# Finding the 32nd score with a padded MAX8, and moving short-lived values into PSUM, in a fused attention, gMLP and MoE kernel

## The chip, the cores and the metric

The kernel runs on one core of one Trainium2 chip. The metric is device time in microseconds (us) of one execution. Engines: TensorE (PE; its weight loads are PEld), VectorE (DVE), ScalarE (ACT), GpSimd (POOL), and SyncE (SP), which only issues DMAs here.

## The reference, cut to what matters

```python
# attention: 2 batches, 8 heads, 576 positions, head dimension 64, all float32
scores = scale * np.matmul(q, k.transpose(0, 1, 3, 2))
kth = np.partition(scores, -32, axis=-1)[..., -32:-31]     # the 32nd largest of each row
scores = np.where(scores >= kth, scores, -1e9)
attn = exp(scores - max); attn = attn / (attn.sum(-1) + 1e-9)
x = (attn @ v)                                  # heads joined: (2, 576, 512)
# gMLP
h = gelu_tanh(x @ w_in); u, v = halves of h
v_s = einsum('ts,bsd->btd', w_sg, layernorm(v) * g_ln) + b_sg     # the "spread"
x = x + (u * v_s) @ w_out
# MoE: each token is sent to one of 8 experts, out = p[e] * relu(x @ w1[e]) @ w2[e]
```

What this case is about is `kth`: for each of 18,432 score rows the kernel needs the 32nd largest value, as the threshold of a mask.

## The kernel before, in words

The work of attention is cut into 72 **units**: a unit is 128 score rows of one head against all 576 keys (or 64 rows each of two heads). `body` walks the row tiles of batch 0 and then of batch 1; `unit` does one unit: `scores` (PE, L307, evacuated by ACT at L310 to `s_sb`), `weights_fast` (the top 32 and the softmax numerators), five transposes on PE (L377), their evacuation on ACT (L380), and ten half-products with V on PE (L385). After every unit `pump` places some steps of the other work in between, taken first in, first out from a list: the eight loads of `w_in` (`load_mlp`, `from_double`), then for every finished row tile the first gMLP product (`mlp_in`), then `spread(0)`, the loads of `w_out`, and the output steps. What is left of the list runs after the last unit. `experts` follows. A planner orders each engine's instructions at build time by priority and by its own estimates of time; on the chip each engine takes them in that order. There are three PSUM banks under the name `m_ps`, taken in turn by all of the work in between.

**The 32nd score, per unit (`weights_fast`).** DVE takes the top 8 of each of eight segments of 72 scores (L336), and then three rounds of MAX8 on the 64 candidates (L339), two MATCH_REPLACE8 between them (L341). The third round is `last8`, whose last value is the 24th score t. ACT takes the sign of t minus each score (L347), which leaves on the side a sum `cnt` = 576 - 2n, with n the number of scores at or above t (24 to 31 when all is well). POOL multiplies score by sign (L351): positive only for positive scores below t. DVE takes MAX8 of those (L353, tile `tb`), the 25th and following scores. The 32nd is the (32-n)th of these eight. DVE picks it (L356): it compares `cnt` with eight constants in `order`, multiplies the matches with `tb`, and sums into `kths`. This is one SCALAR_TENSOR_TENSOR with an accumulator, so that a DVE_READ_ACCUMULATOR follows. The mask is then made on DVE (L364, every other unit), or on ACT with a one-element DVE instruction ahead of it (L361, L362), and multiplied into the exponentials on POOL (L365).

**The weights (`from_double`, L187 on).** `w_in` and `w_out` arrive as 64-bit floats, in 12 pieces of 128 x 512. A piece lands in the raw tile `dbl` (one buffer). DVE shifts and joins the high and low words into a float32 magnitude (L194, L195) in an SBUF tile named `rest`, whose three buffers the units use too; ACT takes the absolute value (L196) and the sign of the high word (L197); POOL multiplies the two (L198).

**The spread.** `spread` evacuates a PSUM bank with one DVE instruction into an SBUF tile `vs` (L533) and multiplies `vs` into U (L537, and L542 for the rows that both batches share).

After attention, two DVE instructions (L1074, L1075) collect flags, over all 72 units, for rows in which the shortcut did not find the threshold; were one set, attention and the experts would be done again exactly, at the end.

Of the kernel before, what the change touches and what calls it, by code (L numbers as in the profile page):

```python
# [11 lines left out]
F32 = mybir.dt.float32  # L12
F32R = mybir.dt.float32r
BF16 = mybir.dt.bfloat16
I32 = mybir.dt.int32
U32 = mybir.dt.uint32
AF = mybir.ActivationFunctionType
OP = mybir.AluOpType
# [25 lines left out]
def tile_topk_gmlp_moe(  # L44
# [15 lines left out]
    nc = tc.nc  # L60
    B, H, D, S = qT.shape
    P = 128
    DM = H * D
# [3 lines left out]
    E, _, FE = w1.shape  # L67
    CE = FE // P
    TOP = 32
    NJ = (S + P - 1) // P  # L70
    LAST = S - (NJ - 1) * P
    HS = S // 2
# [11 lines left out]
    const = ctx.enter_context(tc.tile_pool(name="const", bufs=1))  # L84
# [67 lines left out]
    SEG = 8  # L152
    UNITS = B * (H * (NJ - 1) + H // 2)
    NG = 24
    order = const.tile([P, 8], F32, name="order")


    nc.vector.tensor_scalar(order, iota_e, 2.0, float(S - 2 * (TOP - 1)), op0=OP.mult, op1=OP.add)
    last8 = const.tile([P, UNITS, 8], F32, name="last8")
    kths = const.tile([P, UNITS], F32, name="kths")  # L160

    LESS = 1.0 + 2.0 ** -20

    def attention(fast):
# [21 lines left out]
        def from_double(dst, src):  # L186


            n = dst.shape[-1]
            hl = raw.tile([P, 2 * n], U32, name="dbl", bufs=1)  # L190
            nc.sync.dma_start(hl, src.bitcast(U32))
            l, h = hl[:, 0::2], hl[:, 1::2]
            a = wk.tile([P, n], U32, name="rest", bufs=3)
            nc.vector.tensor_scalar(a, h, 0x08000000, 3, op0=OP.bitwise_xor, op1=OP.logical_shift_left)  # L194
            nc.vector.scalar_tensor_tensor(a, l, 29, a, op0=OP.logical_shift_right, op1=OP.bitwise_or)  # L195
            nc.scalar.activation(a.bitcast(F32), a.bitcast(F32), AF.Abs)  # L196
            nc.scalar.activation(dst, h.bitcast(F32), AF.Sign)  # L197
            nc.gpsimd.tensor_tensor(dst, a.bitcast(F32), dst, op=OP.mult)  # L198

        def load_in(hf, c):  # L200
            from_double(w_in_sb[:, c, hf * F2:(hf + 1) * F2], w_in[c * P:(c + 1) * P, hf * F2:(hf + 1) * F2])
# [109 lines left out]
            return s_sb  # L311

        def weights_exact(s_sb):
            top = sm.tile([P, TOP], F32, name="top")
            rest = wk.tile([P, S], F32, name="rest", bufs=3)
            cur = s_sb
            for r in range(TOP // 8):
                t8 = top[:, r * 8:r * 8 + 8]
                nc.vector.max(t8, cur)
                if r < TOP // 8 - 1:  # L320
                    nc.vector.match_replace(rest, t8, cur, -3.0e38)
                    cur = rest
            nm = sm.tile([P, 1], F32, name="nm")
            nc.vector.tensor_scalar(nm, top[:, 0:1], -scale, None, op0=OP.mult)
            e_sb = wk.tile([P, S], F32, name="e_sb", bufs=5)
            nc.scalar.activation(e_sb, s_sb, AF.Exp, bias=nm, scale=scale)
            nc.vector.scalar_tensor_tensor(e_sb, s_sb, top[:, TOP - 1:TOP], e_sb, op0=OP.is_ge, op1=OP.mult)
            return e_sb

        def weights_fast(s_sb, un):  # L330


            w = S // SEG
            cand = sm.tile([P, 8 * SEG], F32, name="cand", bufs=4)
            for g in range(SEG):
                nc.vector.max(cand[:, 8 * g:8 * g + 8], s_sb[:, g * w:(g + 1) * w])  # L336
            for r in range(NG // 8):
                t8 = last8[:, un, :] if r == NG // 8 - 1 else sm.tile([P, 8], F32, name="ta", bufs=12)
                nc.vector.max(t8, cand)  # L339
                if r < NG // 8 - 1:  # L340
                    nc.vector.match_replace(cand, t8, cand, -3.0e38)  # L341
                if r == 0:
                    nm = sm.tile([P, 1], F32, name="nm")
                    nc.gpsimd.tensor_scalar(nm, t8[:, 0:1], -scale, None, op0=OP.mult)  # L344
            sg = wk.tile([P, S], BF16, name="sg", bufs=3)
            cnt = sm.tile([P, 1], F32, name="cnt")
            nc.scalar.activation(sg, s_sb, AF.Sign, bias=last8[:, un, 7:8], scale=-LESS, accum_out=cnt)  # L347
            e_sb = wk.tile([P, S], F32, name="e_sb", bufs=5)
            nc.scalar.activation(e_sb, s_sb, AF.Exp, bias=nm, scale=scale)  # L349
            below = wk.tile([P, S], F32, name="rest", bufs=3)  # L350
            nc.gpsimd.tensor_tensor(below, s_sb, sg, op=OP.mult)  # L351
            t8 = sm.tile([P, 8], F32, name="tb")
            nc.vector.max(t8, below)  # L353
            pick = sm.tile([P, 8], F32, name="pick")
            kth = kths[:, un:un + 1]
            nc.vector.scalar_tensor_tensor(pick, order, cnt, t8, op0=OP.is_equal, op1=OP.mult, accum_out=kth)  # L356
            mask = wk.tile([P, S], BF16, name="mask", bufs=2)
            if MASK[un % len(MASK)] == "a":

                ink = sm.tile([P, 1], F32, name="ink")  # L360
                nc.vector.tensor_scalar(ink, kth, -(1.0 - 2.0 ** -24), None, op0=OP.mult)  # L361
                nc.scalar.activation(mask, s_sb, AF.Sign, bias=ink)  # L362
            else:
                nc.vector.tensor_scalar(mask, s_sb, kth, None, op0=OP.is_ge)  # L364
            nc.gpsimd.tensor_tensor(e_sb, e_sb, mask, op=OP.mult)  # L365
            return e_sb
# [59 lines left out]
        def mlp_in(t):  # L426
# [13 lines left out]
            def v(c):  # L440
# [7 lines left out]
                with tc.high_priority(offset=EVAC):  # L448
                    vg = one.tile([P, F2], F32, name="row", bufs=3)
                    gelu = nc.scalar.activation(vg, ps["v"], AF.Gelu_apprx_tanh)  # L450
                    with tc.issue_after(gelu.ins):
                        nc.scalar.activation(UT[b][:, :, k * P:(k + 1) * P], ps["u"], AF.Gelu_apprx_tanh)
                    st = sm.tile([P, 6], F32, name="st")
                    nc.vector.bn_stats(st, vg)
                    mv = sm.tile([P, 2], F32, name="mv")
                    nc.vector.bn_aggr(mv, st)
                    ve = sm.tile([P, 1], F32, name="ve")
                    nc.vector.tensor_scalar(ve, mv[:, 1:2], 1e-6, None, op0=OP.add)
                    rs = sm.tile([P, 1], F32, name="rs")
                    nc.gpsimd.tensor_tensor(rs, ve, neghalf, op=OP.pow)  # L460
                    nc.vector.tensor_scalar(VN[b][:, k, :], vg, mv[:, 0:1], rs, op0=OP.subtract, op1=OP.mult)

# [49 lines left out]
        def spread(b):  # L512
# [3 lines left out]
            def step(f, n, j):  # L516
# [12 lines left out]
                if j != js[-1]:  # L529
                    return  # L530
                with tc.high_priority(offset=EVAC):
                    vs = one.tile([P, HS], F32, name="vs", bufs=2)
                    nc.vector.scalar_tensor_tensor(vs, ps[0], g_sb[:, f:f + 1], b_sg_sb[:, at], op0=OP.mult, op1=OP.add)  # L533
                    at = slice(at.start, min(at.stop, FULL))
                    m = at.stop - at.start
# [23 lines left out]

        def logits(b, fill, spare):  # L560

            added = raw.tile([P, 2 * DM], U32, name="dbl", bufs=1).bitcast(F32)[:E + 1, :S]
            both = slice(b * LAST, (b + 1) * LAST)
            for at, u in ((slice(FULL), UT[b]), (slice(FULL, S), UT[B][:, :, both])):
                ps = ps_m.tile([P, 512], F32, name="m_ps")
# [499 lines left out]
                give(slice(0, P), tq, pq)  # L1065
        own.close()

    zero = const.tile([1, DM], F32, name="zero")
    nc.vector.memset(zero, 0.0)
    nc.sync.dma_start(xrows[0:1], zero)  # L1070
    attention(True)

    fa = const.tile([P, UNITS], F32, name="fa")
    nc.vector.tensor_scalar(fa, kths, 1e-30, None, op0=OP.is_le)  # L1074
    nc.vector.scalar_tensor_tensor(fa, last8[:, :, 7], 0.0, fa, op0=OP.is_le, op1=OP.max)  # L1075
    fs = const.tile([P, 1], BF16, name="fs")
    nc.vector.tensor_reduce(fs, fa, axis=AX.X, op=OP.max)
    fi = const.tile([P, 1], I32, name="fi")
# [46 lines left out]
```

## Time and profile before

| | |
|---|---|
| three runs | 612.41, 610.81, 605.28 us; median 610.81 us |
| the profiled execution | 611.23 us, of which the span of instructions is 609.5 us |
| busy in the span | PE 551.0 us (90%), DVE 373.0 (61%), ACT 308.3 (51%), POOL 292.6 (48%) |
| mean granted clock of TensorE | 0.917 of 2.4 GHz |

The shares are means over stages that differ: attention with the work in between runs to about 350 us, the rest of the gMLP to about 440 us, and the experts from there to the end. PE's share includes time at half clock, and instructions that are recorded as busy while the engine is fed slowly.

### The profile page before, as it was taken

The numbers are of one execution on the slowest core, as the hardware profiler recorded it, in microseconds if no ns is written. First come the engines' busy times: TensorE is split into PE (matmuls) and PEld (weight loads), VectorE is DVE, ScalarE is ACT, GpSimd is POOL, SyncE is SP. The second block draws the span as 40 slices with busy tenths as digits, with TensorE's granted clock in tenths as the row PEclk, the third lists the DMA queues.
The fourth block names the chain that finished last, engine by engine and source line by source line (L and its number), as shares of the span: only waits on it lengthen the run. The fifth ranks groups of instructions, "written<-read, shape, count | busy, mean of one in ns | idle before, by whom it ended". The sixth has DMA issues, their size and how long they took to land. (4 is left out here: it accounts for less than half of the span.)

```text
span 609.5 us, 10453 instructions
## 1 busy us (share of the span) xinstructions
PE 551.0 (90%) x3430; PEld 458.6 (75%) x3430; DVE 373.0 (61%) x1765; ACT 308.3 (51%) x563; POOL 292.6 (48%) x330
## 2 busy tenths in 40 slices
PE   6778799999989969898897799999989999999993
PEld 3445667777778768767886478777768999999993
DVE  5889978898989999899899931234800111111110
ACT  3767756978989797866789523323010101111110
POOL 4488948676998858777567820170040102000010
PEclk9555758989999999999898799999999999999998
DMA  9963200000301101210020030000389998766001
GB/s 234 245 169 131 70 27 9 6 24 0 92 19 54 27 17 28 70 35 18 2 70 1 35 114 8 18 2 0 105 274 388 388 387 313 270 236 242 17 18 32
DMA packets 45668, 63.92 MB, mean 105 GB/s; under 512 B 14553, under 2 KB 20697, under 8 KB 45602
## 3 DMA queue, kind: packets, MB, share of 16 engines
q1 hardware_dynamic: 43938, 58.16, 29.6%
q0 software_dynamic: 1664, 4.97, 2.4%
q8 instruction: 30, 0.49, 0.3%
q14 instruction: 36, 0.29, 0.2%
HBM read 56.04 MB, written 7.33 MB: 104 GB/s over the span
## 5 line engine op out<-in xcount | busy, mean ns | idle before, releaser
L385 PE MATMUL pv<-v,pt 128*128 128x96 f32 (+1 forms) x720 | 113.2, 296 | 9.8 <-DVE row L401 6.0
L385 PEld LDWEIGHTS pv<-v,pt 128*128 128x128 f32 x720 | 106.7, 215 | 19.9 <-DVE row L401 7.3
L365 POOL TENSOR_TENSOR e_sb<-e_sb,mask 128x576 f32<-128x576 f32 x72 | 94.0, 1307 | 42.0 <-ACT e_sb L349 14.4
L351 POOL TENSOR_TENSOR rest<-s_sb,sg 128x576 f32<-128x576 f32 x72 | 93.1, 1297 | 20.6 <-ACT sg L347 19.8
L336 DVE MAX8 cand<-s_sb 128x8 f32<-128x72 f32 x576 | 89.6, 217 | 19.6 <-ACT s_sb L310 19.3
L307 PE MATMUL s_ps<-kk,qh 64*128 64x288 f32 (+1 forms) x224 | 80.4, 474 | 15.1 <-ACT s_sb L310 15.0
L377 PE MATMUL pt_ps<-ident,e_sb 128*128 128x128 f32 x360 | 73.6, 297 | 8.5 <-ACT pt L380 5.2
L968 PE MATMUL h_ps<-xw,w_sb 128*128 128x152 f32 (+6 forms) x512 | 76.5, 298 | 0.8 <-DMA w_sb<-in_w_dram 0.8
L979 PE MATMUL y_ps<-hT,w_sb 128*128 128x152 f32 (+6 forms) x512 | 75.3, 299 | 0.7 <-DMA w_sb<-in_w_dram 0.7
L968 PEld LDWEIGHTS h_ps<-xw,w_sb 128*128 128x128 f32 x512 | 71.4, 190 | 1.1 <-ACT hT L971 1.1
L979 PEld LDWEIGHTS y_ps<-hT,w_sb 128*128 128x128 f32 x512 | 71.0, 190 | 1.1 <-DMA w_sb<-in_w_dram 1.1
L307 PEld LDWEIGHTS s_ps<-kk,qh 64*128 64x128 f32 (+1 forms) x224 | 43.9, 224 | 32.7 <-ACT s_sb L310 21.6
L377 PEld LDWEIGHTS pt_ps<-ident,e_sb 128*128 128x128 f32 x360 | 51.8, 164 | 19.7 <-issue 11.0
L971 ACT ACTIVATE hT<-h_ps 128x152 f32<-128x152 f32 (+6 forms) x32 | 9.7, 302 | 112.7 <-PE h_ps L968 111.9
L347 ACT ACTIVATE sg<-s_sb,last 128x576 bf16<-128x576 f32 x72 | 55.6, 772 | 18.4 <-DVE last L339 14.0
L380 ACT ACTIVATE pt<-pt_ps 128x640 f32<-128x640 f32 x72 | 50.4, 700 | 25.4 <-PE pt_ps L377 24.4
L940 POOL DMA_INDIRECT out_dram<-orow,to x10 | 10.0, 1000 | 103.1 <-ACT orow L939 48.3
L349 ACT ACTIVATE e_sb<-s_sb,nm 128x576 f32<-128x576 f32 x72 | 55.7, 773 | 2.2 <-POOL nm L344 1.2
L310 ACT ACTIVATE s_sb<-s_ps 128x576 f32<-128x576 f32 x72 | 46.3, 642 | 18.6 <-PE s_ps L307 18.5
L973 DVE TENSOR_SCALAR hT<-h_ps 128x152 f32<-128x152 f32 (+6 forms) x32 | 10.3, 323 | 73.2 <-PE h_ps L968 67.7
L353 DVE MAX8 tb<-rest 128x8 f32<-128x576 f32 x72 | 53.6, 745 | 1.2 <-POOL rest L351 1.1
L981 DVE COPY yT<-y_ps 128x152 f32<-128x152 f32 (+6 forms) x32 | 9.9, 323 | 64.2 <-PE y_ps L979 64.2
(248 smaller groups left out, 919.7 us busy)
## 6 DMA issues: line engine op xcount, KB each, us to landing
w_sb<-in_w_dram SPq DMA_DIRECT2D x32, 1024.0 KB, 12.3
dbl<-in_w_in_dram SPq DMA_DIRECT2D x8, 512.0 KB, 4.6
kr<-in_kT_dram SPq DMA_DIRECT2D x16, 144.0 KB, 3.2
v<-in_v_dram SPq DMA_DIRECT2D x8, 256.0 KB, 5.4
dbl<-in_w_out_dram SPq DMA_DIRECT2D x4, 512.0 KB, 3.5
xin<-row SPq DMA_DIRECT2D x8, 256.0 KB, 2.3
qraw<-in_qT_dram SPq DMA_DIRECT2D x16, 128.0 KB, 2.8
back<-xin SPq DMA_DIRECT2D x8, 256.0 KB, 2.7
```

Of the source, the lines that this page charges most:

```text
L307: nc.tensor.matmul(s_ps[:, n, :HS], w, k[:, n * HS:(n + 1) * HS], start=m == 0, stop=m == len(terms) - 1)
L336: nc.vector.max(cand[:, 8 * g:8 * g + 8], s_sb[:, g * w:(g + 1) * w])
L347: nc.scalar.activation(sg, s_sb, AF.Sign, bias=last8[:, un, 7:8], scale=-LESS, accum_out=cnt)
L349: nc.scalar.activation(e_sb, s_sb, AF.Exp, bias=nm, scale=scale)
L351: nc.gpsimd.tensor_tensor(below, s_sb, sg, op=OP.mult)
L353: nc.vector.max(t8, below)
L365: nc.gpsimd.tensor_tensor(e_sb, e_sb, mask, op=OP.mult)
L377: tr = nc.tensor.transpose(pt_ps[:, t * P:(t + 1) * P], p_sb[:, k0:k0 + P], ident)
L380: nc.scalar.activation(pt.rearrange("p t q -> p (t q)"), pt_ps[:, :NJ * P], AF.Relu)
L385: nc.tensor.matmul(PV[b][:, i % g, :], pt[:, t, :], V1[b][:, t, w * i * (D + 1):w * i * (D + 1) + nv], start=t == 0, stop=t == NJ - 1)
L968: nc.tensor.matmul(hp[:, :W], w1_sb[:, c, f * P:(f + 1) * P], xw[:, c, at], start=c == 0, stop=c == CD - 1)
L979: nc.tensor.matmul(yp[:, :W], w2_sb[:, f, c * P:(c + 1) * P], hT[:, f, :W], start=f == 0, stop=f == CE - 1)
```

## The change

Five things change.

1. The pick goes. `rest` is seven columns wider; POOL writes into them (cnt + order) x -2^100, with `order` now 2i - 527, so that exactly n - 24 of the seven come out huge and positive, and the others negative. The eighth value of DVE's MAX8 over all 583 columns is then the 32nd score itself. `cnt` is kept for every unit, in `cnts`.
2. In `from_double` the joined words go to a PSUM bank of `m_ps` instead of an SBUF `rest`; ACT writes the absolute value straight to the destination, and the sign in place over the low words of the raw tile, with a stride of two.
3. `dbl` has two buffers. Some small tiles get fewer buffers.
4. `vs` is not a tile of its own any more: the evacuation of the spread writes into its PSUM bank in place, and the product with U reads it there.
5. The row of zeros is written from 128 partitions with 4 values each instead of one partition with 512. The flags get five more DVE instructions on 72 columns, since the pick did one of the tests on the way.

```diff
-    order = const.tile([P, 8], F32, name="order")
-    nc.vector.tensor_scalar(order, iota_e, 2.0, float(S - 2 * (TOP - 1)), op0=OP.mult, op1=OP.add)
+    ADD = TOP - NG - 1
+    order = const.tile([P, ADD], F32, name="order")
+    nc.vector.tensor_scalar(order, iota_e[:, :ADD], 2.0, float(2 * NG + 1 - S), op0=OP.mult, op1=OP.add)
     last8 = const.tile([P, UNITS, 8], F32, name="last8")
-    kths = const.tile([P, UNITS], F32, name="kths")
+    next8 = const.tile([P, UNITS, 8], F32, name="next8")
+    cnts = const.tile([P, UNITS], F32, name="cnts")
...
-            hl = raw.tile([P, 2 * n], U32, name="dbl", bufs=1)
+            hl = raw.tile([P, 2 * n], U32, name="dbl", bufs=2)
             nc.sync.dma_start(hl, src.bitcast(U32))
             l, h = hl[:, 0::2], hl[:, 1::2]
-            a = wk.tile([P, n], U32, name="rest", bufs=3)
+            a = ps_m.tile([P, n], F32, name="m_ps").bitcast(U32)
             nc.vector.tensor_scalar(a, h, 0x08000000, 3, op0=OP.bitwise_xor, op1=OP.logical_shift_left)
             nc.vector.scalar_tensor_tensor(a, l, 29, a, op0=OP.logical_shift_right, op1=OP.bitwise_or)
-            nc.scalar.activation(a.bitcast(F32), a.bitcast(F32), AF.Abs)
-            nc.scalar.activation(dst, h.bitcast(F32), AF.Sign)
-            nc.gpsimd.tensor_tensor(dst, a.bitcast(F32), dst, op=OP.mult)
+            nc.scalar.activation(dst, a.bitcast(F32), AF.Abs)
+            sign = l.bitcast(F32)
+            nc.scalar.activation(sign, h.bitcast(F32), AF.Sign)
+            nc.gpsimd.tensor_tensor(dst, dst, sign, op=OP.mult)
...
-                t8 = last8[:, un, :] if r == NG // 8 - 1 else sm.tile([P, 8], F32, name="ta", bufs=12)
+                t8 = last8[:, un, :] if r == NG // 8 - 1 else sm.tile([P, 8], F32, name="ta", bufs=8)
...
-            cnt = sm.tile([P, 1], F32, name="cnt")
+            cnt = cnts[:, un:un + 1]
             nc.scalar.activation(sg, s_sb, AF.Sign, bias=last8[:, un, 7:8], scale=-LESS, accum_out=cnt)
...
-            below = wk.tile([P, S], F32, name="rest", bufs=3)
-            nc.gpsimd.tensor_tensor(below, s_sb, sg, op=OP.mult)
-            t8 = sm.tile([P, 8], F32, name="tb")
-            nc.vector.max(t8, below)
-            pick = sm.tile([P, 8], F32, name="pick")
-            kth = kths[:, un:un + 1]
-            nc.vector.scalar_tensor_tensor(pick, order, cnt, t8, op0=OP.is_equal, op1=OP.mult, accum_out=kth)
+            below = wk.tile([P, S + ADD], F32, name="rest", bufs=3)
+            nc.gpsimd.tensor_tensor(below[:, :S], s_sb, sg, op=OP.mult)
+            nc.gpsimd.tensor_scalar(below[:, S:], order, cnt, -2.0 ** 100, op0=OP.add, op1=OP.mult)
+            nc.vector.max(next8[:, un, :], below)
+            kth = next8[:, un, 7:8]
...
-                    vs = one.tile([P, HS], F32, name="vs", bufs=2)
+                    vs = ps[0]
                     nc.vector.scalar_tensor_tensor(vs, ps[0], g_sb[:, f:f + 1], b_sg_sb[:, at], op0=OP.mult, op1=OP.add)
...
-            added = raw.tile([P, 2 * DM], U32, name="dbl", bufs=1).bitcast(F32)[:E + 1, :S]
+            added = raw.tile([P, 2 * DM], U32, name="dbl", bufs=2).bitcast(F32)[:E + 1, :S]
...
-    zero = const.tile([1, DM], F32, name="zero")
+    zero = const.tile([P, DM // P], F32, name="zero")
     nc.vector.memset(zero, 0.0)
-    nc.sync.dma_start(xrows[0:1], zero)
+    nc.sync.dma_start(xrows[0:1].rearrange("o (p f) -> p (o f)", p=P), zero)
     attention(True)
     fa = const.tile([P, UNITS], F32, name="fa")
-    nc.vector.tensor_scalar(fa, kths, 1e-30, None, op0=OP.is_le)
+    nc.vector.tensor_scalar(fa, next8[:, :, 7], 1e-30, None, op0=OP.is_le)
     nc.vector.scalar_tensor_tensor(fa, last8[:, :, 7], 0.0, fa, op0=OP.is_le, op1=OP.max)
+    fc = const.tile([P, UNITS], I32, name="fc")
+    nc.vector.tensor_scalar(fc, cnts, float(2 * TOP - 2 - S), None, op0=OP.add)
+    nc.vector.scalar_tensor_tensor(fa, fc, float(2 * ADD), fa, op0=OP.is_gt, op1=OP.max)
+    nc.vector.scalar_tensor_tensor(fa, fc, 0.0, fa, op0=OP.is_lt, op1=OP.max)
+    nc.vector.tensor_scalar(fc, fc, 1, None, op0=OP.bitwise_and)
+    nc.vector.tensor_tensor(fa, fa, fc, op=OP.max)
```

Left out of the diff: `top` and the four small tiles of the layer norm go from 6 buffers to 3, and the exact path takes its `rest` from the wider tile.

## Rows read from the trace of the kernel before

**Rows 1.** Windows view by stage; columns are named in the first line.

```profile
core 0: us, PE busy (x) PEld busy (x) DVE busy (x) ACT busy (x) POOL busy (x), PEclk, DMA share, GB/s
20.00:80.00 60.00, 49.37 (x167) 35.45 (x167) 53.49 (x232) 42.27 (x77) 48.00 (x46) 0.56 0.51 134
80.00:100.00 20.00, 20.00 (x86) 15.52 (x87) 14.74 (x82) 10.84 (x19) 10.19 (x12) 0.63 0.05 16
100.00:340.00 240.00, 213.75 (x1421) 177.41 (x1420) 224.71 (x1140) 198.53 (x354) 178.35 (x187) 0.97 0.10 31
340.00:440.00 100.00, 98.54 (x572) 73.56 (x570) 45.92 (x150) 26.58 (x49) 26.21 (x23) 0.98 0.12 38
```

**Rows 2.** Lines view, whole span: xcount | busy us, mean ns | idle before, releaser.

```profile
L356 DVE SCALAR_TENSOR_TENSOR pick<-order,cnt,tb 128x8 f32<-128x8 f32 x72 | 40.1, 557 | 0.6
L356 DVE DVE_READ_ACCUMULATOR pick<-order,cnt,tb 128x1 f32 x72 | 5.6, 78 | 0.0
...
L353 DVE MAX8 tb<-rest 128x8 f32<-128x576 f32 x72 | 53.6, 745 | 1.2 <-POOL rest L351 1.1
...
L336 DVE MAX8 cand<-s_sb 128x8 f32<-128x72 f32 x576 | 89.6, 217 | 19.6 <-ACT s_sb L310 19.3
```

**Rows 3.** Source views of four DVE lines: duration in ns, min/median/max.

```profile
L356 DVE SCALAR_TENSOR_TENSOR pick<-order,cnt,tb x72: 198/437/1341, 18.7 to 350.6; 128x8 f32<-128x8 f32 x72
...
L364 DVE TENSOR_SCALAR mask<-s_sb,kths x36: 482/508/1637, 20.0 to 349.3; 128x576 bf16<-128x576 f32 x36
...
L533 DVE SCALAR_TENSOR_TENSOR vs<-m_ps,g_sb,b_sg_sb x16: 493/506/518, 262.1 to 421.5; 128x288 f32<-128x288 f32 x16
...
L537 DVE TENSOR_TENSOR ut<-ut,vs x16: 369/450/1559, 263.4 to 422.1; 128x288 f32<-128x288 f32 x8, 128x224 f32<-128x224 f32 x8
```

**Rows 4.** Windows view of L356 alone (pick and its accumulator read).

```profile
20.00:100.00 80.00, 7.28 (x28) 0.57 0.39 104
100.00:340.00 240.00, 29.87 (x106) 0.97 0.10 31
```

**Rows 5.** Lines view: the joining of weight words, and a PSUM read of equal width.

```profile
L195 DVE SCALAR_TENSOR_TENSOR rest<-dbl,rest 128x512 uint32<-128x512 uint32 x12 | 12.7, 1055 | 0.0
...
L194 DVE TENSOR_SCALAR rest<-dbl 128x512 uint32<-128x512 uint32 x12 | 9.8, 814 | 5.3 <-DMA dbl<-in_w_in_dram 4.0 <-DMA dbl<-in_w_out_dram 1.3
...
L220 DVE COPY back<-m_ps 128x512 f32<-128x512 f32 x4 | 2.7, 677 | 0.4 <-PE m_ps L218 0.4
```

**Rows 6.** Windows view of L194 alone.

```profile
20.00:100.00 80.00, 6.25 (x7) 0.57 0.39 104
```

**Rows 7.** Timeline of DVE: one joining of words with nothing holding its first instruction.

```profile
62.33 0.42 DVE L194 TENSOR_SCALAR rest<-dbl 128x512 uint32<-128x512 uint32 x1
```

**Rows 8.** Lines view: three groups of POOL.

```profile
L351 POOL TENSOR_TENSOR rest<-s_sb,sg 128x576 f32<-128x576 f32 x72 | 93.1, 1297 | 20.6 <-ACT sg L347 19.8 <-DVE tb L353 0.5
...
L344 POOL TENSOR_SCALAR nm<-ta 128x1 f32<-128x1 f32 x72 | 20.4, 284 | 23.3 <-DVE ta L339 19.8 <-DVE ink L361 1.9 <-DVE rc L392 1.2
...
L460 POOL TENSOR_TENSOR rs<-ve,neghalf 128x1 f32<-128x1 f32 x9 | 5.5, 610 | 33.1 <-DVE ve L458 33.1
```

**Rows 9.** Windows view in two stretches where POOL is fullest.

```profile
60.00:80.00 20.00, 15.66 (x70) 12.71 (x70) 18.48 (x75) 14.11 (x26) 18.49 (x18) 0.67 0.21 72
160.00:180.00 20.00, 18.39 (x131) 15.64 (x130) 17.48 (x85) 17.62 (x31) 19.44 (x19) 1.00 0.22 64
```

**Rows 10.** Waits view: SyncE's queue (us in total, times, longest us).

```profile
SPq L191 <- DVE rest L195: 36.1, 10, 7.4
```

**Rows 11.** Lines view: the second flag instruction.

```profile
L1075 DVE SCALAR_TENSOR_TENSOR fa<-last,fa 128x72 f32<-128x72 f32 x1 | 1.4, 1364 | 0.0
```

**Rows 12.** Windows view around the rise of the clock.

```profile
88.00:92.00 4.00, 4.00 (x13) 2.62 (x12) 1.74 (x13) 2.89 (x6) 0.49 (x2) 0.50 0.00 0
...
96.00:100.00 4.00, 4.00 (x29) 3.33 (x28) 3.26 (x13) 2.73 (x5) 2.88 (x3) 1.00 0.04 9
```

**Rows 13.** Timeline of SyncE: the store of the row of zeros.

```profile
4.47 0.54 SPq L1070 DMA_DIRECT2D xrows<-zero  x1
```

More of the change, by code (lines that the diff above doesn't have):

```diff
@@ L313, in weights_exact @@
         def weights_exact(s_sb):
-            top = sm.tile([P, TOP], F32, name="top")
-            rest = wk.tile([P, S], F32, name="rest", bufs=3)
+            top = sm.tile([P, TOP], F32, name="top", bufs=3)
+            rest = wk.tile([P, S + ADD], F32, name="rest", bufs=3)[:, :S]
             cur = s_sb
@@ L452, in v @@
                         nc.scalar.activation(UT[b][:, :, k * P:(k + 1) * P], ps["u"], AF.Gelu_apprx_tanh)
-                    st = sm.tile([P, 6], F32, name="st")
+                    st = sm.tile([P, 6], F32, name="st", bufs=3)
                     nc.vector.bn_stats(st, vg)
-                    mv = sm.tile([P, 2], F32, name="mv")
+                    mv = sm.tile([P, 2], F32, name="mv", bufs=3)
                     nc.vector.bn_aggr(mv, st)
-                    ve = sm.tile([P, 1], F32, name="ve")
+                    ve = sm.tile([P, 1], F32, name="ve", bufs=3)
                     nc.vector.tensor_scalar(ve, mv[:, 1:2], 1e-6, None, op0=OP.add)
-                    rs = sm.tile([P, 1], F32, name="rs")
+                    rs = sm.tile([P, 1], F32, name="rs", bufs=3)
                     nc.gpsimd.tensor_tensor(rs, ve, neghalf, op=OP.pow)
```

## The prediction

> **What bounds the kernel now.** I read the windows by stage first [rows 1]. From 440 us on the experts run, which the change doesn't touch. From 340 to 440 PE is busy 98.54 of 100 us and the rest is idle half the time: work taken off DVE is worth almost nothing there. The place to look is 100 to 340. DVE is the fullest engine, 224.71 of 240 us (93.6%), then PE with 213.75, ACT 198.53, POOL 178.35. From 20 to 100 DVE has 53.49 + 14.74 = 68.23 of 80 us and PE 49.37 + 20.00 = 69.37, but PE's time is at a mean granted clock of 0.57 [rows 4], near the lower of its two levels: the same work at full clock would be far shorter.
>
> Then the lines of DVE [rows 2] and, since a mean hides it, the spread of durations [rows 3]. The pick handles 8 elements, takes 198 ns at best and 557 on average, up to 1341. The mask (482 to 1637) and the product with `vs` (369 to 1559) spread as widely. But the evacuation of the spread, one input in PSUM, stays between 493 and 518. The long ones end with a POOL multiply, which takes 1297 ns [rows 8]: some DVE forms are held while POOL works in SBUF, and an instruction with a PSUM operand is not. So 557 - 198 = 359 ns of a mean pick is waiting, counted as DVE's busy time.
>
> **The pick.** Removed are 72 x (557 + 78) ns = 45.7 us of DVE [rows 2]; 29.87 lie in 100 to 340 (53 units) and 7.28 in 20 to 100 [rows 4]. Not all of it is won: a DVE mask that came right behind a held pick found POOL's multiply over, and will now meet it itself. In 100 to 340 that is at most 26 masks x 0.359 = 9.5 us, at least 0; I take 4.7. MAX8 grows by seven elements at (745 - 217) / 504 = 1.05 ns each [rows 2]: 53 x 7 ns = 0.4 us.
>
> POOL gets one small instruction per unit, behind the multiply and ahead of MAX8. The trace has no such form. Its lower bound is the mean one-element instruction, 284 ns, its upper the 610 ns of the one-element power; nothing excludes either, and a gain is excluded, since it is only added. It is nearest in kind to the first; six more elements at 1297 / 576 = 2.25 ns make 297 ns [rows 8], over 72 units 21.4 us (43.9 by the upper bound), in 100 to 340 15.7. It waits for `cnt`, which ACT writes right behind the signs, and the multiply ahead of it on POOL hides that. Queued behind it on POOL are the other units' maximum and mask products; DVE's MAX8 waits for it. The chain of one unit gets 0.30 longer there and 0.635 shorter at the pick, so it doesn't grow.
>
> **The weight words.** Twelve pairs cost 814 + 1055 = 1869 ns on average. In PSUM, by the nearest row of 512 elements with a PSUM operand, 677 each [rows 5]: 1354, a gain of 0.515 x 12 = 6.2 us of DVE, 3.6 for the seven from 20 to 100 [rows 6], 2.1 for the four of `w_out`. Against this: the first of the pair, when nothing holds it, takes 0.42 in SBUF [rows 7], so that the move costs it 0.26 us wherever POOL isn't in the way. The Trainium skill says that in "VectorE: DVE Perf Modes", "Why PSUM operands drop a tier": an operand in PSUM takes away the mode that reads one tensor through both SBUF ports. By that alone this part would lose 12 x 0.26 = 3.1 us. I go by the means, because the held case is the usual one here. ACT's two instructions and POOL's product keep their sizes; the strides I bound by 0 and 1 us in all. A bank of `m_ps` is now held for about 2 us per piece. The first eight pieces come before the gMLP needs the banks; the last four don't: 0 to 8 us of PE waiting, and I take 1.
>
> The second raw buffer lets SyncE issue the next piece earlier: its queue stood 36.1 us, in 10 waits, for the joining before [rows 10], with the loads of keys and queries behind it. DVE idled 5.3 us for landing pieces [rows 5]; I count 3 of it as won, all in the front, within 0 and 5.3.
>
> **The rest.** With `vs` in PSUM its product should fall from a median of 450 towards 369 [rows 3], 16 x 0.08 = 1.3 us, up to 10 if all long ones go; half of it falls where DVE is fullest: I take 1. The bank is held longer by that product, hidden by the two other banks. The store of zeros, now 128 pieces, is issued in 0.54 us [rows 13]; nothing reads it before the experts: 0 to 1 us, taken as 0. Five more flag instructions at up to 1.364 us [rows 11] are 6.8 us of DVE just after the last unit, where DVE has 54 idle us [rows 1]; I count 0, and 6.8 if the planner puts them ahead of the last layer norms. Smaller rings of small tiles: 0.
>
> **The sum.** In 100 to 340 DVE loses 29.9 + 2.1 + 1 and gets 4.7 + 0.4: 224.7 - 27.9 = 196.8. ACT stays at 198.5, POOL becomes 178.35 + 15.7 = 194. PE, 213.75, is then the fullest. How full can the fullest engine be in orders fixed at build time? DVE now reaches 93.6%; PE at that share gives 213.75 / 0.936 = 228.4, a gain of 11.6 us (0 if PE's idle time is all latency, 26 if it all goes), less 1 for the banks. In 20 to 100 DVE falls from 68.2 by 7.3 + 3.6, and by 3 of its idle time; PE at 93.6% gives 69.37 / 0.936 = 74.1, a gain of 5.9 (0 to 10.6). Elsewhere 0. Together 16.5 us off the profiled execution's 611.23 (span 609.5, 1.7 around it), which stands 0.4 over the median of 610.81: 594.7 against the former, **594** against the latter. Its own range, with a fair part of both stages open, is 584 to 602.
>
> **Rivals.**
>
> *PE was the bound all along.* Its idle 26 us in 100 to 340 are then the latency of chains over four engines, which a shorter queue on DVE hardly changes, and in front the half clock keeps PE's 69.37 us. For it: PE at 89% is near the top already, and ACT, POOL and DVE come out within 5 us of each other, so that there is no slack engine. Against: DVE idled only 15 of 240 us. Gain 0 to 8 us: 603 to 611.
>
> *The clock rises earlier.* The granted clock is 0.50 from 88 to 92 with PE recorded as busy all the time, and 1.00 from 96 on, when the dense products of the gMLP have begun [rows 12]. If the denser front lets it rise 20 us sooner, 20 us of PE work shrink to 10: 584, range 576 to 590. Against: PE was recorded as full at 0.50. The Trainium skill, "TensorE: Matmul & The Clock Gate", Part 1, has the clock throttled by default and released by sustained activity; that speaks for this rival, and the row of 88 to 92 shows that a recorded busy time isn't enough.
>
> *POOL paces the units (slower).* It is at 18.49 of 20 us in 60 to 80 and 19.44 in 160 to 180 [rows 9]. Were it the bound throughout, the new instruction would add 72 x 0.297 = 21.4 us: 632. It decides from the point where POOL's sum passes PE's: (213.75 - 178.35) / 53 = 0.67 us per unit, above both bounds of the price. Against it, then, on average; for it, those stretches.
>
> *It doesn't do what it says.* Should the new flags trip, attention and experts run again: over 1,100 us. The same tests of sign, count and parity were made by the pick, and the profile shows one pass.
>
> **How the numbers follow.** Forecast 0.53, PE all along 0.29, clock 0.09, POOL 0.08, flags 0.01. Measurement tells 2% from no change: below 598.6 is faster, above 623.0 slower. Of the forecast 0.82 of its chance lies below 598.6, 0.43, and the clock's 0.09 with it: faster 0.52. Same: 0.10 + 0.29 = 0.39. Slower 0.09. The range 578 to 612 takes in the first two rivals but for their edges, and leaves out POOL and the flags.
>
> **What would show it.** No line of the pick; DVE's busy time down by some 45 us, less what masks gain (a median well over 508 ns would be the inherited wait); the joining at about 680 ns each with little spread; a POOL line of 72 at about 0.3 us; DVE below PE in 100 to 340 and PE's share up to 94%. I am wrong if PE's idle time there stays near 26 us, if POOL's new line is far above 0.6 us, or if PE waits for `m_ps` from 240 to 300 us.

## The result and the profile after

The changed kernel takes **605.73 us** (median of 20 runs, 597.15 to 617.60) against 610.39 us (20 runs, 605.28 to 615.15): 4.7 us or 0.8% less, where the forecast was 594 us, 2.7%. The ratio is **0.9867, 95% interval 0.9835 to 0.9898**, a gain of 1.3% or 8.1 us. Ratios, here and below, compare the fast runs alone (those within 1.5% of the fastest of their kernel), medians take all runs. The gain is clear of noise, but below the 2% at which the prediction begins to say faster. The profiled execution took 604.11 us with a span of 602.4 us. The direction was right; 4.7 us by the medians, 8.1 by the ratio, came of 16.5.

The windows view of the changed kernel, by the stages and columns of [rows 1]:

```profile
20.00:80.00 60.00, 51.02 (x202) 36.00 (x200) 53.25 (x285) 49.95 (x96) 56.78 (x67) 0.67 0.55 142
80.00:100.00 20.00, 19.87 (x127) 15.39 (x126) 16.55 (x66) 14.00 (x26) 18.82 (x25) 1.00 0.06 21
100.00:340.00 240.00, 216.84 (x1370) 177.85 (x1371) 205.35 (x996) 190.57 (x340) 189.74 (x232) 0.94 0.10 29
340.00:440.00 100.00, 97.91 (x599) 75.35 (x598) 34.65 (x132) 22.75 (x42) 19.96 (x27) 0.95 0.16 53
```

Read column by column. DVE, the fullest engine from 100 to 340 before, is now at 205.35 us and PE leads, as forecast. But PE is at 90.3% and not 93.6% (it stands idle for 23.2 us there, 26.3 before), and the granted clock has changed sides: in front it rose (1.00 from 80 to 100, where it was 0.63), and from 100 to 340 it fell from 0.97 to 0.94. What that stage lost to the lower clock (one minus the granted clock, summed over windows of 10 us) is 15.3 us of full clock, against 8.2 before.

Its lines view (count | busy us, mean ns | idle before and its releaser), for the lines that the change touches:

```profile
L356 DVE MAX8 next<-rest 128x8 f32<-128x583 f32 x72 | 54.6, 759 | 18.0 <-POOL rest L355 17.5
L365 DVE TENSOR_SCALAR mask<-s_sb,next 128x576 bf16<-128x576 f32 x36 | 31.3, 869 | 1.9 <-POOL e_sb L366 1.7
L355 POOL TENSOR_SCALAR rest<-order,cnts 128x7 f32<-128x7 f32 x72 | 22.2, 308 | 6.3
L196 DVE TENSOR_SCALAR m_ps<-dbl 128x512 uint32<-128x512 uint32 x12 | 8.2, 683 | 2.2 <-DMA dbl<-in_w_out_dram 1.2 <-DMA dbl<-in_w_in_dram 1.0
L197 DVE SCALAR_TENSOR_TENSOR m_ps<-dbl,m_ps 128x512 uint32<-128x512 uint32 x12 | 8.2, 681 | 0.0
L538 DVE TENSOR_TENSOR ut<-ut,m_ps 128x288 f32<-128x288 f32 (+1 forms) x16 | 6.5, 410 | 0.1
L1076 DVE SCALAR_TENSOR_TENSOR fa<-last,fa 128x72 f32<-128x72 f32 x1 | 1.0, 969 | 0.0
```

The pick has no line any more. New is the last number of the first row: DVE stands idle 17.5 us ahead of MAX8 until POOL's small instruction is done; before, MAX8 waited 1.1 us in all for POOL [rows 2]. The source views give the spread, to be read against [rows 3]:

```profile
L365 DVE TENSOR_SCALAR mask<-s_sb,next x36: 501/722/1670, 21.3 to 337.1; 128x576 bf16<-128x576 f32 x36
...
L196 DVE TENSOR_SCALAR m_ps<-dbl x12: 669/680/695, 16.5 to 286.0; 128x512 uint32<-128x512 uint32 x12
...
L355 POOL TENSOR_SCALAR rest<-order,cnts x72: 282/286/571, 17.5 to 335.3; 128x7 f32<-128x7 f32 x72
...
L538 DVE TENSOR_TENSOR ut<-ut,m_ps x16: 361/408/453, 253.3 to 414.3; 128x288 f32<-128x288 f32 x8, 128x224 f32<-128x224 f32 x8
```

With the operand in PSUM the joining and the product lose their long cases (product: maximum 453 ns, was 1559). The mask's median went from 508 to 722 ns: that is what the prediction named as the sign of waits inherited from the pick.

**Where the time went, unit by unit.** The end of ACT's evacuation of the transposes marks when a unit is through. Counted after the first, the changed kernel's 12th unit was through at 97.3 us (108.3 before), the 18th at 120.6 (130.7), the 24th at 151.4 (158.6), the 36th at 210.7 (209.1), the last at 369.6 (381.2). The 12th, the 36th and the last in the timeline of ACT (start us, duration us; the end is their sum), of the changed kernel:

```profile
96.58 0.68 ACT L381 ACTIVATE pt<-pt_ps 128x640 f32<-128x640 f32 x1
...
209.96 0.71 ACT L381 ACTIVATE pt<-pt_ps 128x640 f32<-128x640 f32 x1 [0.59 <-PE pt_ps L378]
...
368.88 0.70 ACT L381 ACTIVATE pt<-pt_ps 128x640 f32<-128x640 f32 x1 [4.33 <-PE pt_ps L378]
```

and of the kernel before:

```profile
107.57 0.68 ACT L380 ACTIVATE pt<-pt_ps 128x640 f32<-128x640 f32 x1
...
208.38 0.68 ACT L380 ACTIVATE pt<-pt_ps 128x640 f32<-128x640 f32 x1
...
380.50 0.70 ACT L380 ACTIVATE pt<-pt_ps 128x640 f32<-128x640 f32 x1 [4.33 <-PE pt_ps L377]
```

So it was 10 to 11 us ahead in front, had lost all of it by 210 us, and won it again later; after that it lost some of it once more (the lead of 11.6 us at the last unit is 7.1 at the end of the span). Roughly by the stages of the forecast: 11.0 us gained in front, where 5.9 were forecast; 0.6 from there to the last unit, where 10.6 were forecast; 4.5 lost behind it, where nothing was forecast. Behind the last unit the granted clock fell once where it had not before. The stretch in the windows views of the changed kernel (first) and of the kernel before:

```profile
380.00:400.00 20.00, 19.87 (x99) 16.13 (x97) 3.84 (x12) 4.99 (x9) 12.37 (x11) 0.76 0.00 1
```

```profile
380.00:400.00 20.00, 20.00 (x124) 15.17 (x124) 4.61 (x16) 6.97 (x12) 5.87 (x6) 1.00 0.04 14
```

That is 0.24 x 20 = 4.8 us of full clock, with PE recorded as busy nearly all the time; why it fell there is open.

One of the places where it fell back, in the timeline of all engines (start us, duration us, engine, line; in brackets the idle time before and its releaser):

```profile
162.17 0.77 DVE L356 MAX8 next<-rest 128x8 f32<-128x583 f32 x1 [1.37 <-POOL rest L355]
...
163.53 1.50 DVE L365 TENSOR_SCALAR mask<-s_sb,next 128x576 bf16<-128x576 f32 x1 [0.27 <-POOL e_sb L366]
...
166.54 0.27 PE L378 MATMUL pt_ps<-ident,e_sb 128*128 128x128 f32 x1
...
167.45 0.43 PE L310 MATMUL s_ps<-kk,ql 128*128 128x288 f32 x2
...
168.41 0.22 DVE L342 MAX8 last<-cand 128x8 f32<-128x64 f32 x1
168.54 0.16 DVE L457 BATCH_NORM_AGGREGATE mv<-st 128x2 f32<-128x6 f32 x1
...
168.74 0.77 ACT L350 ACTIVATE sg<-s_sb,last 128x576 bf16<-128x576 f32 x1 [3.22 <-DVE mv L457]
169.42 0.19 ACT L350 ACTIVATION_READ_ACCUMULATOR sg<-s_sb,last 128x1 f32 x1
169.51 0.68 ACT L381 ACTIVATE pt<-pt_ps 128x640 f32<-128x640 f32 x1
...
170.25 1.35 PE L386 MATMUL pv<-v,pt 128*128 128x96 f32 x10 [2.38 <-ACT pt L381]
```

Read it backwards. PE waits 2.38 us for the evacuated transposes, whose last it had finished at 166.81. ACT is free (it sat idle 3.22 us), but its order has the signs of another unit ahead of that evacuation, and the signs wait for `last` from DVE (the profile names `mv`, DVE's record right behind it). DVE is late: it stood 1.37 us ahead of MAX8 for POOL's small instruction, and then a mask took 1.50 us, three times its best. A fixed order carried one engine's wait over two others into PE. Then the clock, in the windows view of the same place:

```profile
164.00:168.00 4.00, 3.87 (x32) 3.40 (x30) 3.86 (x16) 1.09 (x2) 3.75 (x5) 1.00 0.24 66
168.00:172.00 4.00, 1.75 (x15) 1.66 (x15) 1.53 (x6) 3.23 (x5) 3.76 (x6) 0.98 0.00 0
172.00:176.00 4.00, 2.90 (x13) 2.59 (x12) 3.98 (x16) 3.54 (x7) 3.84 (x5) 0.50 0.00 0
```

Full clock up to the gap, the lower level behind it. From 100 us on PE had three gaps of this size, ending at 131.5, 170.2 and 207 us (2.3, 2.4 and 3.0 us); within 2 us of each end began a stretch at half clock, of 10.2, 6.8 and 6.8 us.

### The profile page after: what moved, and what is told of

The parts are those of the page before. It is cut to its first block, busy times and chain, and to the rows that moved or that the text cites. A ratio compares the mean times of both kernels' runs of the same rounds, so it can differ in the third digit from the quotient of the medians.

```text
span 602.4 us, 10412 instructions
## 1 busy us (share of the span) xinstructions
PE 548.9 (91%) x3430; PEld 458.6 (76%) x3430; DVE 341.4 (57%) x1626; ACT 306.2 (51%) x563; POOL 311.1 (52%) x402
## 5 line engine op out<-in xcount | busy, mean ns | idle before, releaser
L386 PE MATMUL pv<-v,pt 128*128 128x96 f32 (+1 forms) x720 | 111.9, 292 | 9.0 <-DVE row L402 4.5
L386 PEld LDWEIGHTS pv<-v,pt 128*128 128x128 f32 x720 | 105.1, 211 | 17.1 <-ACT pt L381 7.5
L354 POOL TENSOR_TENSOR rest<-s_sb,sg 128x576 f32<-128x576 f32 x72 | 93.9, 1305 | 13.5 <-ACT sg L350 12.6
L339 DVE MAX8 cand<-s_sb 128x8 f32<-128x72 f32 x576 | 87.7, 218 | 18.0 <-ACT s_sb L313 17.7
L310 PE MATMUL s_ps<-kk,qh 64*128 64x288 f32 (+1 forms) x224 | 79.0, 467 | 15.3 <-ACT s_sb L313 15.2
L378 PE MATMUL pt_ps<-ident,e_sb 128*128 128x128 f32 x360 | 76.0, 302 | 8.0 <-ACT pt L381 3.8
L356 DVE MAX8 next<-rest 128x8 f32<-128x583 f32 x72 | 54.6, 759 | 18.0 <-POOL rest L355 17.5
```

The costliest lines, as they stand in the source:

```text
L310: nc.tensor.matmul(s_ps[:, n, :HS], w, k[:, n * HS:(n + 1) * HS], start=m == 0, stop=m == len(terms) - 1)
L354: nc.gpsimd.tensor_tensor(below[:, :S], s_sb, sg, op=OP.mult)
L356: nc.vector.max(next8[:, un, :], below)
L378: tr = nc.tensor.transpose(pt_ps[:, t * P:(t + 1) * P], p_sb[:, k0:k0 + P], ident)
L386: nc.tensor.matmul(PV[b][:, i % g, :], pt[:, t, :], V1[b][:, t, w * i * (D + 1):w * i * (D + 1) + nv], start=t == 0, stop=t == NJ - 1)
```

## The experiments

Each was timed in five rounds against the kernel before on the same chip. Medians in us; ratios to before, with their 95% interval, in brackets. In the five sets of runs the median of before was 610.2 to 611.8. The changed kernel in its own order was timed beside the kernel before, not beside its other orders.

### One part at a time

`pick_only` is before with part 1 alone, the flags that it needs and some shorter rings of small tiles. `rest_only` is the changed kernel with the pick put back (parts 2 to 5). `append_dve` and `no_append` change one line of the changed kernel:

```diff
 append_dve
-nc.gpsimd.tensor_scalar(below[:, S:], order, cnt, ...)
+nc.vector.tensor_scalar(below[:, S:], order, cnt, ...)
 no_append
-nc.gpsimd.tensor_scalar(below[:, S:], order, cnt, ...)
-nc.vector.max(next8[:, un, :], below)
+nc.vector.max(next8[:, un, :], below[:, :S])
```

> The kernel before with the padded MAX8 in place of the pick and nothing else of the change (a few rings of tiny tiles shortened to make room). Two theories of why only 4.7 of 16.5 us came. Theory C (chains and clock): DVE was full in the middle but its order was not what set the pace; its freed time becomes idle time, PE keeps its gaps, and a gap drops PE's clock for 7 to 10 us. It expects 604 to 609 us, DVE at least 25 us less busy, and half-clock time between 100 and 340 us at or above the 8.2 us lost there before. Theory P (POOL): the new POOL instruction ahead of MAX8 eats what the pick gave back. It expects 609 to 615.

> The changed kernel with the pick put back: words and spread values in PSUM, two raw buffers, the zeros, but no padded MAX8 and no new POOL instruction. Theory C: most of the gain is in front (weight words, DMA waits), which this keeps: 603 to 608 us, lost clock from 20 to 100 us clearly under the 34.0 us of before. Theory P: better than the changed kernel, since the POOL instruction is gone: 596 to 602.

> The changed kernel with the seven appended values made on DVE instead of POOL. DVE gets 72 x about 0.14 us = 10 us, POOL loses 22 us. Theory C: the same as the changed kernel within 3 us, 602 to 609. Theory P: at least 8 us better than the changed kernel, 594 to 598.

> The changed kernel without the appended values: MAX8 reads 576 columns and its eighth value is taken as it is, so that the threshold is too low in rows with more than 24 scores at or above t; nothing else is left out. Theory C: 600 to 606 us, less than 5 us better than the changed kernel. Theory P: 592 to 598.

Measured: `pick_only` 599.50 (0.9788 [0.9739, 0.9836]); `rest_only` 614.51 (1.0045 [1.0011, 1.0079]); `append_dve` 614.11 (1.0052 [1.0014, 1.0090]); `no_append` 586.42 (0.9515 [0.9463, 0.9566]). All four came out outside the ranges of both theories. The first part alone is faster than the whole change, and the other four together are no gain, though they take work off DVE. `append_dve` puts the small instruction on DVE; its source views:

```profile
L355 DVE TENSOR_SCALAR rest<-order,cnts x72: 205/583/1461, 16.6 to 343.3; 128x7 f32<-128x7 f32 x72
...
L362 DVE TENSOR_SCALAR ink<-next x36: 125/135/153, 25.9 to 346.9; 128x1 f32<-128x1 f32 x36
```

It is held just like the pick it replaces: 50 of the 72 take over 300 ns, and in the trace each of these ends 24 to 31 ns behind the end of an instruction of POOL. From 100 to 340 DVE is as full as it was before the change, 226.66 of 240 us:

```profile
100.00:340.00 240.00, 211.64 (x1370) 175.27 (x1371) 226.66 (x1051) 192.85 (x343) 173.73 (x183) 0.95 0.09 27
```

and the gain is gone. That fits a kernel paced by what DVE carries per unit, but the edit changes the order too, so this run alone doesn't show it. Without the appended values the change is worth 24.0 us by the medians, 29.6 by the ratio, more than I forecast for the whole. From 100 to 340, `no_append`:

```profile
100.00:340.00 240.00, 223.53 (x1475) 180.07 (x1475) 212.65 (x1045) 198.57 (x355) 182.91 (x191) 0.99 0.12 37
```

PE reaches 93.1% at a clock of 0.99, near the 93.6% of the forecast, but with less work on POOL, without the wait of MAX8 for it, and in another order.

### Load on POOL, or DVE's wait for it?

`aside` lets POOL make the seven values, but into a tile that nothing reads. `nm_dve` moves POOL's one-element product (minus the maximum) to DVE, which takes 17 us of work off POOL and leaves MAX8's wait; `pick_nm_dve` is that on `pick_only`. `planned` is `aside` and was to place MAX8 behind POOL's instruction in the planner's order only, with no wait on the chip.

```diff
 aside
-nc.gpsimd.tensor_scalar(below[:, S:], order, cnt, ...)
-nc.vector.max(next8[:, un, :], below)
+aside = sm.tile([P, ADD], F32, name="aside", bufs=2)
+nc.gpsimd.tensor_scalar(aside, order, cnt, ...)
+nc.vector.max(next8[:, un, :], below[:, :S])
 nm_dve, pick_nm_dve
-nc.gpsimd.tensor_scalar(nm, t8[:, 0:1], -scale, None, op0=OP.mult)
+nc.vector.tensor_scalar(nm, t8[:, 0:1], -scale, None, op0=OP.mult)
 planned (on aside; app and mx are POOL's and DVE's instructions)
+tc.add_manual_dep(mx.ins, app.ins.name, DependencyInfo(NoSync, DATA))
```

> As without the appended values, but POOL makes them all the same, into a tile of their own that nothing reads: POOL's 22 us are back, the wait of MAX8 for them is not. (The threshold is again the plain eighth value.) Theory L (load): what costs 19 us is POOL's time, 72 instructions in its queue; 602 to 608 us. Theory W (wait): what costs is MAX8 standing behind the instruction; 584 to 591 us.

> The changed kernel with the one-element instruction for minus the maximum moved from POOL to DVE: POOL loses 72 x 0.236 = 17 us, DVE gets 72 x about 0.14 = 10 us, MAX8 still waits for the appended values. Theory L: 588 to 595 us. Theory W: 603 to 612 us.

> The padded MAX8 alone (599.5 us) with minus the maximum made on DVE. Theory L: 584 to 592 us, the best version so far. Theory W: 598 to 606 us.

> The aside kernel (POOL makes the seven values, nothing reads them, MAX8 over 576 columns), with an order drawn for the planner alone: it plans MAX8 behind POOL's instruction as in the changed kernel, and on the chip MAX8 doesn't wait for it. Theory W (the wait on the chip costs): 584 to 592 us, like aside. Theory R (the plan that the wait leads to costs): 598 to 607 us, like the changed kernel.

Measured: `aside` 586.82 (0.9614 [0.9567, 0.9660]); `nm_dve` 593.11 (0.9706 [0.9650, 0.9762]); `pick_nm_dve` 596.08 (0.9755 [0.9709, 0.9800]); `planned` 590.61 (0.9652 [0.9595, 0.9709]). POOL's extra work alone costs little: `aside` keeps it and is 0.4 us slower than `no_append` by the medians, 6.0 by the ratios, where theory L put it at 602 to 608 us. That speaks for the wait. But `nm_dve` keeps the wait and is 12.6 us faster than the changed kernel, in the range of theory L, and `pick_nm_dve` lies between the two ranges; so the wait alone doesn't explain it either.

`planned` did not become what it was meant to be. In its trace DVE, ACT and POOL take their instructions (1626, 563 and 402) in the same order as in `aside`, and PE loads its weights in the same order too, while DVE's order in the changed kernel parts from it at the 80th instruction. So `planned` says nothing of the plan; it is a second series of `aside`, 3.8 us from the first. Each of the other edits makes the planner build another order, and that had to be priced by itself.

### The same instructions in another order

`RATE` is the work, in us by the planner's own estimate, that `pump` places between units, for each row tile. Changing it leaves every instruction as it is and moves only the order:

```diff
-RATE = (2.0, 2.0, 2.0, 2.0, 2.0, 2.4, 2.4, 2.4, 2.2, 2.2)
+RATE = (2.0, 2.1, 2.1, 2.1, 2.1, 2.4, 2.4, 2.4, 2.2, 2.2)   # reroll
+RATE = (2.0, 2.2, 2.2, 2.2, 2.2, 2.5, 2.5, 2.5, 2.2, 2.2)   # reroll2
+RATE = (2.0, 2.3, 2.3, 2.3, 2.3, 2.4, 2.4, 2.4, 2.2, 2.2)   # reroll3
```

`reroll` and the names that begin with `after` are the changed kernel, those with `before` the kernel before, the others the kernels above, at these rates.

> The changed kernel with the rate at which work in between is placed in batch 0 raised from 2.0 to 2.1 after the first tile: the same instructions, another plan. Theory R (the plan): differences of 10 to 20 us between variants are the planner's luck; it expects a move of 6 us or more either way from 605.7. Theories L and W both expect 602 to 609 us.

> The aside kernel with the placing rate of batch 0 at 2.1, another plan for the same instructions. If the plan's luck is small against 19 us, this stays within 6 us of 586.8; theory R in its plain form (luck) allows 595 and more.

> The kernel before with the same other rate, another plan. Within 6 us of 610.4 if luck is small; a move of 8 us or more would mean that the 4.7 us between before and after is within the plan's luck.

> The changed kernel with rates 2.2 in batch 0 and 2.5 in batch 1, a third plan of it (605.7 and 600.6 us so far). Within 598 to 609 us if luck is some 5 us; theory R allows 590 to 615.

> The kernel before with the rates of after_reroll2 (2.2 and 2.5). Theory R (the changed kernel's own plan is an unlucky one, and the change itself is worth what was forecast): 606 to 614 us, so that like plans differ by about 18 us. If the rates themselves are what is good: 594 to 602.

> The changed kernel with the pick put back, at these rates. If the pick is the whole of the gain: 606 to 616 us, as rest_only (614.5). If parts 2 to 5 gain too under a better plan: 598 to 605.

> The padded MAX8 alone, at these rates. If the pick is the whole of the gain: within 6 us of after_reroll2's 592 us, 588 to 600. If parts 2 to 5 carry part of it: 600 to 606.

> The changed kernel with minus the maximum on DVE, at these rates: both steps that gained. 580 to 590 us if their gains add up, 590 to 596 if each only found a better plan.

> The kernel before with 2.3 in batch 0 after the first tile and batch 1 as it was: a fourth plan (610.4, 612.9, 625.8 so far). Theory R: 605 to 626 us.

> The changed kernel with the same rates: a fourth plan (605.7, 600.6, 592.0 so far). Theory R, the change worth some 17 us over plans and the plan's luck added to it: 590 to 606 us, and 8 to 26 us below before_reroll3. If the 4.7 us are the change's true worth: within 9 us of before_reroll3.

Of these ten, `before_reroll`, `after_reroll2`, `before_reroll3` and the time of `after_reroll3` fell into a range named ahead; the other six lie outside of all (`rest_reroll2` by 0.3 us). Measured, medians, in the order of the four rates; the last row is the difference of the two ratios, times 610.4 us:

| | own | reroll | reroll2 | reroll3 |
|---|---|---|---|---|
| before | 610.39 | 612.85 (1.0048 [1.0011, 1.0085]) | 625.76 (1.0303 [1.0254, 1.0352]) | 624.69 (1.0188 [1.0126, 1.0251]) |
| changed | 605.73 | 600.62 (0.9835 [0.9774, 0.9897]) | **591.98 (0.9719 [0.9667, 0.9770])** | 597.23 (0.9772 [0.9724, 0.9820]) |
| difference | 4.7 | 12.2 | 33.8 | 27.5 |
| by the ratios | 8.1 | 13.0 | 35.6 | 25.4 |

| | own | reroll2 |
|---|---|---|
| before | 610.39 | 625.76 |
| part 1 alone | 599.50 | 612.90 (0.9983 [0.9934, 1.0032]) |
| parts 2 to 5 alone | 614.51 | 605.27 (0.9907 [0.9869, 0.9945]) |
| all parts | 605.73 | 591.98 |

Further, `aside_reroll` 594.12 (0.9704 [0.9642, 0.9765]), and `nm_reroll2` 598.84 (587.38 to 600.52, no ratio, since its runs scattered).

Three readings. **First**, at equal rates the change is worth 4.7, 12.2, 33.8 and 27.5 us, 19.5 on average (20.5 by the ratios). The 16.5 forecast lie within one standard error of that, 6.7 us, which is too wide to call them confirmed. An equal rate is not an equal order, either: the rate the kernel came with is the best of the four for before and the worst of the four for the changed kernel. Best against best it is 18.4 us, and `after_reroll2` beats both kernels. **Second**, part 1 gains in every pair: 10.9 and 8.8 us at the old rate, 12.9 and 13.3 at the other (by the ratios 12.9, 10.9, 19.5 and 11.5). Parts 2 to 5 don't: they lose 4.1 and 6.2 us at the old rate and win 20.5 and 20.9 at the other (by the ratios -2.7, -4.8, 24.2 and 16.1). Each of these sets one order against one other, while orders of the same instructions lie up to 15 us apart, so that what a part is worth stays uncertain. **Third**, the wait: three orders without it gave 586.4 (`no_append`), 588.7 (`aside` and `planned` together) and 594.1 (`aside_reroll`), 589.7 on average; the four orders with it 605.7, 600.6, 592.0 and 597.2, 598.9 on average. The difference is 9.2 us with a standard error of 3.7 from these scatters, and it is uneven: 17 to 19 us at the old rate, 6.5 at `reroll`'s. So the versions with the wait are slower; whether by the wait itself or by the orders that the planner builds around it is not shown, as no run has the order of the changed kernel without the wait.

What the order does is seen where `after_reroll2` and the changed kernel part. They keep pace up to the 18th unit (119.9 and 120.6 us); at the 36th it is 198.5 against 210.7. The windows of `after_reroll2`:

```profile
100.00:340.00 240.00, 220.46 (x1445) 177.84 (x1446) 208.72 (x1000) 193.06 (x345) 193.16 (x234) 0.99 0.12 37
120.00:210.00 90.00, 81.07 (x545) 68.20 (x543) 77.97 (x387) 78.16 (x137) 79.65 (x98) 0.96 0.13 36
```

and the second stretch in the changed kernel:

```profile
120.00:210.00 90.00, 78.91 (x486) 66.29 (x487) 67.85 (x331) 71.35 (x126) 72.86 (x89) 0.88 0.11 31
```

Same instructions, and the one has 0.04 x 90 = 3.6 us of full clock lost in it, the other 10.8: 7.2 of the 12.2 us by which they part up to the 36th unit. Over 100 to 340 it is 3.4 against 15.3 us: 11.9, where their last units lie 11.1 us apart (358.5 and 369.6). Each of the two is a single execution. The longest single wait of PE for evacuated transposes is 1.4 us in `after_reroll2` and 3.0 in the changed kernel.

## Why the prediction was right in direction and wrong in size

**The step that failed is "The sum"**, and in it the sentence that PE would reach DVE's 93.6% share: "PE at that share gives 213.75 / 0.936 = 228.4, a gain of 11.6 us". It took the order of instructions for given. The change makes the planner build a new one, and in this one PE reached 90.3%, at a clock of 0.94: from the 12th unit to the last, 0.6 us came of the 11.6 less 1. The sign of being wrong that I had named came with it, PE's idle time near 26 us (23.2). None of the other three orders of the same instructions reached 93.6% either: `reroll` 89.7%, `after_reroll2` 91.9% and `after_reroll3` 91.1%, at clocks of 0.96, 0.99 and 0.98. So the share that one engine reaches in one order said nothing certain of another engine in another. What the order moves, up to 13.7 us between 605.73 and 591.98 and largely with the clock in the two executions compared, is as much as the largest term of the sum, and no term of mine stood for it. In the split by parts it shows in parts 2 to 5: I gave them some 3 us of gain, and they measured 4 to 6 us of loss in this order, 20 of gain in another. Part 1 measured 9 to 13 us where the sum gave it some 13 (of 27.9 us of DVE in the middle it is 24.8, of 13.9 in front 7.3; these shares of 11.6 and 5.9).

**POOL's new instruction, costed at nothing on the path.** Its duration was right (297 forecast, 308 measured) and its load costs little, as `aside` shows. "So it doesn't grow" was wrong in what it left out: I counted the 0.30 us into the chain of one unit, not that MAX8 stands in DVE's order with other units' work behind it. DVE idled 17.5 us there, and the timeline above shows one such wait arriving at PE. By the seven orders above, the versions with the wait are some 9 us slower; how much of it is the wait itself is open.

**The pick.** A size was off, without consequence for the sum, in which PE was then the fullest. I took 45.7 us from the sum of durations, 29.87 of it from 100 to 340. Records of neighbours overlap: DVE's busy time of before without the pick's records is 342.3 us over the span (30.7 less) and 202.3 from 100 to 340 (22.4 less). Put that in place of 29.87 and DVE should come to 204.3 us; it came to 205.35. The masks' inherited waits, taken at 4.7 us there, came to 4.6 over the whole span (their upper bound, 26 x 0.359, is 9.3 and not 9.5 us). The rows that the pick served are 72 x 128 = 9,216, half of the 18,432 named at the start.

**The weight words** held: 683 + 681 ns were forecast as 2 x 677, a gain of 6.0 us of DVE. The rule of the Trainium skill that I set against it ("VectorE: DVE Perf Modes", "Why PSUM operands drop a tier") agrees with the best case, 0.42 us in SBUF [rows 7] against 0.68 now. By it alone the sum has the wrong sign, because the SBUF form was held by POOL to a mean of 814 and 1055 ns [rows 5] and the PSUM form never (669 to 695). With the second raw buffer DVE's idle time for landing pieces fell from 5.3 to 2.2 us, the 3 that I counted. For the weight pieces the banks of `m_ps` held PE up for nothing that its waits show. For the product they did, once, which I had called hidden by the other banks. PE's waits (us in total, times, longest us), the changed kernel first, then the kernel before:

```profile
PE m_ps L509 <- DVE ut L538: 1.4, 1, 1.4
```

```profile
PE m_ps L508 <- DVE vs L533: 0.3, 1, 0.3
```

The product itself lost its long cases and gained 16 x 0.25 = 4.0 us, where I took 1 and bounded it by 10; the bound was too wide, since all long cases gone are 16 x (0.660 - 0.369) = 4.7 us.

**The front** gained more than forecast, 10 to 11 us instead of 5.9, and by the rival to which I gave 0.09: the clock from 20 to 100 was granted at 0.67 and 1.00 (mean 0.75), before at 0.57. `rest_only` shows 0.69 there and `pick_only` 0.70, so either half of the change makes part of it. It is luck, not forecast, that these 5 us more make up for the 4.5 us lost behind the last unit, where the sum has "Elsewhere 0".

**The rivals.** *PE was the bound all along* names the time that came (603 to 611) but not the cause: with the same instructions PE gives 592. *POOL paces the units* is excluded by `aside`, which keeps POOL's work and takes 586.82 us. The flags' instructions ran from 334.5 to 341.2 us, where DVE was full (7.61 of 8 us from 334 to 342) but PE, busy for all of the 8 us, did not wait for them; the longest took 0.97 us where 1.36 was the bound [rows 11].

**Open.** Whether the changed kernel is systematically better at more work between units, or four orders are only four draws; whether the rate that the kernel came with had been picked for the kernel before, which would favour the change at all other rates; what the wait costs in an order that stays the same; and why `nm_dve` gains 12.6 us at the old rate with the wait in place, when `nm_reroll2` isn't faster than `after_reroll2`. The 12.6 us are no more than orders of the same instructions differ by.

## What to carry to other kernels

Where a planner builds the order, an edit is two changes, the work and the order; here the same instructions span 13.7 us and the kernel before 15.4, more than the change was worth as delivered. The share of the fullest engine before is not a share that the next one will reach: none of four orders had it. So time more than one order of each version before a difference of a few us is put down to the edit. Price a small instruction by what stands behind its reader in that reader's queue, not by its own duration, and take a line's worth from the engine's busy time without it, not from the sum of its durations.

## What the runs showed of the hardware

- A DVE TENSOR_SCALAR of 128x7 with its per-partition scalar in SBUF is held while POOL works (205 to 1461 ns, mean 665; 50 of 72 over 300 ns, each ending 24 to 31 ns behind an instruction of POOL), the one-element form on DVE is not (125 to 153 ns). So the wait takes neither a second full tensor nor a long instruction.
- Gaps of PE of 2.3 to 3.0 us in the changed kernel were each followed by 6.8 to 10.2 us at the lower clock level, 3.4 to 5.1 us of full clock: each gap cost more behind it than in it. That is no rule. In the kernel before, a gap of 2.52 us that ended at 290.7 us was followed by 0.39 x 4 + 0.04 x 4 = 1.7 us of full clock lost:

```profile
288.00:292.00 4.00, 0.91 (x7) 0.53 (x5) 4.00 (x21) 3.57 (x7) 3.01 (x5) 1.00 0.00 0
292.00:296.00 4.00, 3.64 (x19) 3.62 (x20) 3.20 (x18) 1.58 (x4) 1.96 (x2) 0.61 0.00 0
296.00:300.00 4.00, 4.00 (x38) 4.00 (x37) 3.27 (x21) 2.74 (x6) 2.19 (x4) 0.96 0.02 6
```

- The Trainium skill, "TensorE: Matmul & The Clock Gate", Part 1, ties the full clock to sustained activity; the rows at 168 to 176 us agree, and the row at 380 to 400 us, with the clock at 0.76 and PE busy for 19.87 of 20 us, shows that a recorded busy time isn't enough.
